# A spectral layer and a bilinear GLU on one core: where the first stage's odd folds run, and when its remaining features are split

## The chip, the cores and the metric

The kernel runs on one core of a Trainium2 chip. Its engines are TensorE (PE; PEld is its weight load), VectorE (DVE), ScalarE (ACT), GpSimd (POOL) and SyncE (SP), which issues most transfers. Each engine works through its own queue in order and meets the others through semaphores. The metric is the device time of one launch in microseconds (us); before the change it is 720.43 us, the median of 3 runs (720.38 to 720.56).

## The reference

`x` is 2048 rows of 640 float32 values. With `ln` a layer norm over the 640 values of a row (no gain, no bias):

```python
h   = x + irfft2(rfft2(ln(x)) * (w_r + 1j * w_i))       # w_r, w_i: 2048 x 321
h2  = h + ((ln(h) @ w_gate) * (ln(h) @ w_up)) @ w_down   # 640 x 1728, 1728 x 640
```

The first line is a global filter: a two-dimensional Fourier transform over rows and columns, a product with a learned complex filter, and the way back. The second is a gated unit without a nonlinearity.

## The kernel before, in words

The 2048 rows are 128 times 16: row 16p + t stands on partition p of tile t, so a tile (`XP[t]`, 640 values and one of padding) holds 128 rows, and there are 16 of them (`NT`). The transform over rows is split in the same way, into a 128-point part inside a tile and a 16-point part across tiles; the transform over the 640 columns uses its symmetry, so that columns are first added to and subtracted from their mirror images ("folds"), twice.

**Stage 1** (the loop at L262 to L292) goes over the tiles t = 0 to 15. For each tile:

- `odd(t)`, L178 to L181: 320 differences of mirrored columns, by GpSimd, from the raw tile. They need no layer-norm statistics, because a difference loses the mean.
- `even(t)`, three VectorE operations: L190 (322 sums of mirrored columns less twice the mean), L194 (66 second folds) and L195 (320 second folds). The last two read what `odd` and L190 wrote. The results lie in one of four slots of `fold` (`NR` = 4), so the folds of tile t + 4 wait until tile t's are used.
- `scale_c(t)`, L214: the 128 x 128 transform table times the rows' inverse deviation, by VectorE (by ScalarE for tile 0, L212).
- `s1_mm(t)`, L200 to L207: TensorE multiplies the folds with that table. Four blocks of 128 features go to one PSUM bank (L206), of which there are two in turn; the fifth block, the remaining features, goes to another (L207).
- The next turn of the loop reads the banks out: `s1_main` (L225, ScalarE) copies the four blocks; `s1_hi` (L220, ScalarE) writes the fifth block rounded to float32r into `s1r[:, 0]`, and `s1_lo` (L229, VectorE) the difference from the unrounded value into `s1r[:, 1]`.

The layer-norm statistics of tiles 0, 2, 3 and 6 to 9 are VectorE's (`bn_stats` at L131 and L132, `bn_aggr` at L133, two small operations at L137 and L138 for a group), those of tiles 1, 4, 5 and 10 to 15 ScalarE's (L146 and L147, then L149 on VectorE). After each group come a root on ScalarE (L156) and four small VectorE operations (L157 to L160) that give the inverse deviation. Lists say at which tile each operation is issued: `dve[t]` is zipped between the operations of `even(t)`, `acts[t]` follows `s1_hi` in ScalarE's queue, and `post[t]` holds the root. The order within every queue is the order of these calls; no planner changes it.

GpSimd's `odd(t + 1)` is issued in the turn of tile t, behind a one-element copy `hold` (L287) in the first two turns. `hold` reads the last element that L195 writes, so that the fold behind it starts when L195 of that turn is over.

**Stage 2** (from L315) takes 16 groups g (eight of the 128 outputs, from every tile): `d_mm(g)` multiplies the four main blocks (`s1`) and then the split fifth block (`s1r[:, 0]` twice, then `s1r[:, 1]`) with the column tables, `d_out(g)` (ScalarE, L328 to L331) copies the result, `s2_mm(g)` (L340) does the 16-point part, and VectorE's `filt(g)` multiplies with the filter. The filter and table loads on SP's queue follow these steps. The inverse transform, the second layer norm and the gated unit come after, with TensorE nearly always at work.

Of the kernel before, what the change touches and what calls it, by code (L numbers as in the profile page):

```python
# [11 lines left out]
F32 = mybir.dt.float32  # L12
F32R = mybir.dt.float32r
AF = mybir.ActivationFunctionType
OP = mybir.AluOpType

P = 128
S, D, NF, FF = 2048, 640, 321, 1728
NT = S // P
NG = 16  # L20
# [2 lines left out]
FW = (160, 193, 161, 161)  # L23
FOFF = (0, 160, 353, 514)
NR = 4
ON_ACT = (1, 4, 10, 14)
EPS = 1e-5


def view(t, offset, dims):  # L30
    return bass.AP(tensor=t.tensor, offset=t.offset + offset, ap=[list(t.ap[0])] + [list(d) for d in dims])


def f32(ap):
    return ap.bitcast(F32)


def zipped(main, side):
    n = len(main)
    for i, f in enumerate(main):  # L40
        f()
        for h in side[i * len(side) // n:(i + 1) * len(side) // n]:
            h()
# [3 lines left out]
def tile_spectral_glu(ctx: ExitStack, tc: tile.TileContext, x, wf, wgu, wlast, wdown, wdlast,  # L47
                      cc, ci, fmain, frem, imain, irem, mm, out):
    nc = tc.nc
# [3 lines left out]
    small = ctx.enter_context(tc.tile_pool(name="small", bufs=4))  # L53
    ctx.enter_context(tc.manual_schedule())

    tt, act = nc.vector.tensor_tensor, nc.scalar.activation
# [3 lines left out]
    def banks(key, name):  # L60
        if key in pools:
            open_pools[key].close()
        open_pools[key] = ExitStack()
        pools[key] = open_pools[key].enter_context(tc.tile_pool(name=name, bufs=2, space=bass.MemoryType.PSUM))
# [26 lines left out]
    XP = [keep.tile([P, D + 1], F32, name=f"x{t}") for t in range(NT)]  # L91
# [4 lines left out]
    def home(tag, shape, name, dt=F32):  # L96
        return keep.tile(shape, dt, tag=tag, name=name)
# [8 lines left out]
    frt = home("dA", [P, 2, 2, NQ], "frt", F32R)  # L106
    s1 = home("big", [P, 4, NG, P], "s1")
    s1r = home("wA", [P, 2, NG, P], "s1r", F32R)
    fold = home("qm", [P, NR * 1026 + 2 * D], "fold")
    wts = home("wB", [P, 3, 2, 2, NQ], "wts")  # L110
    bits = home("dB", [P, 2560], "bits")
# [9 lines left out]
    def moments(ts, junk=None, total=None):  # L121
        n = len(ts)
        m2 = small.tile([P, n], F32, tag="m2", name="m2")
        ve = small.tile([P, n], F32, tag="ve", name="ve")
        if junk is None:
            mv = small.tile([P, n, 2], F32, tag="mv", name="mv")

            def one(t, i):
                st = small.tile([P, 2, 6], F32, tag="st", name="st")
                return [  # L130
                    lambda: nc.vector.bn_stats(st[:, 0], X[t][:, 0:320]),  # L131
                    lambda: nc.vector.bn_stats(st[:, 1], X[t][:, 320:640]),  # L132
                    lambda: nc.vector.bn_aggr(mv[:, i], st),  # L133
                ]

            fs = [f for i, t in enumerate(ts) for f in one(t, i)]
            fs.append(lambda: nc.vector.tensor_scalar(m2, mv[:, :, 0], 2.0, None, op0=OP.mult))  # L137
            fs.append(lambda: nc.vector.tensor_scalar(ve, mv[:, :, 1], EPS, None, op0=OP.add))  # L138
            return m2, ve, fs
        sq = small.tile([P, n], F32, tag="sq", name="sq")  # L140
        fs = []
        if total is not None:
            fs.append(lambda: nc.vector.tensor_scalar(m2, total, 2.0 / D, None, op0=OP.mult))
        for i, t in enumerate(ts):
            if total is None:
                fs.append(lambda t=t, i=i: act(junk[i], X[t], AF.Identity, scale=2.0 / D, accum_out=m2[:, i:i + 1]))  # L146
            fs.append(lambda t=t, i=i: act(junk[i], X[t], AF.Square, bias=m2[:, i:i + 1], scale=-2.0,  # L147
                                           accum_out=sq[:, i:i + 1]))
        fs.append(lambda: nc.vector.tensor_scalar(ve, sq, 0.25 / D, EPS, op0=OP.mult, op1=OP.add))  # L149
        return m2, ve, fs  # L150
# [14 lines left out]
    def front(ts):  # L165
        n = len(ts)
        r = small.tile([P, n], F32, tag="r", name="r")
        junk = [fold[:, o:o + D] for o in (NR * 1026, NR * 1026 + D)]
        m2, ve, fs = moments(ts, junk * 2 if ts[0] in ON_ACT else None)
        for i, t in enumerate(ts):  # L170
            SC[t] = r[:, i:i + 1], m2[:, i:i + 1]
        return fs, inverse_root(ve, r, n)

    def folded(t):
        o = t % NR * 1026
        return fold[:, o:o + 642], fold[:, o + 642:o + 1026]

    def odd(t):  # L178
        f = folded(t)[0]
        nc.gpsimd.tensor_tensor(view(f, 0, [[160, 2], [1, 160]]), view(XP[t], 1, [[320, 2], [1, 160]]),  # L180
                                view(XP[t], 639, [[-320, 2], [-1, 160]]), op=OP.subtract)  # L181

    def even(t):
        f, j = folded(t)

        def both(n):
            return view(f, 0, [[320, 2], [1, n]]), view(f, 160, [[321, 2], [1, n]])

        return [
            lambda: nc.vector.scalar_tensor_tensor(view(f, 320, [[161, 2], [1, 161]]),  # L190
                                                   view(XP[t], 0, [[320, 2], [1, 161]]), SC[t][1],
                                                   view(XP[t], 640, [[-320, 2], [-1, 161]]),
                                                   op0=OP.subtract, op1=OP.add),
            lambda: tt(view(j, 33, [[-33, 2], [1, 33]]), *both(33), op=OP.add),  # L194
            lambda: tt(view(j, 64, [[1, 2], [2, 160]]), *both(160), op=OP.subtract),  # L195
        ]

    PS1, CR = {}, {}
# [10 lines left out]
    def scale_c(t):  # L209
        CR[t] = crs[t % 4]  # L210
        if t == 0:
            act(CR[t], cct, AF.Copy, scale=SC[t][0])  # L212
        else:
            nc.vector.tensor_scalar(CR[t], cct, SC[t][0], None, op0=OP.mult)  # L214

    def at(base, t):
        return view(base, 4 * t, [[64, 32], [1, 4]])

    def s1_hi(t):
        act(at(s1r[:, 0], t), PS1[t][1][:, 0:P].rearrange("p (g m) -> p g m", g=32), AF.Copy)  # L220

    def s1_main(t):
        n = 4 if t < NT - 1 else 2
        for c in range(0, 4, n):
            act(view(s1, 4 * t + 2048 * c, [[2048, n], [64, 32], [1, 4]]),  # L225
                PS1[t][0][:, c * P:(c + n) * P].rearrange("p (c g m) -> p c g m", c=n, g=32), AF.Copy)

    def s1_lo(t):
        tt(at(s1r[:, 1], t), PS1[t][1][:, 0:P].rearrange("p (g m) -> p g m", g=32), f32(at(s1r[:, 0], t)),  # L229
           op=OP.subtract)  # L230

    banks("a", "pone")
    dve = [[] for _ in range(NT)]
    acts = [[] for _ in range(NT)]
    post = {}

    def spread(fs, where, a, b):
        n = b - a + 1
        for k, f in enumerate(fs):
            t = a + k * n // len(fs)  # L240
            where[max(0, t)].append(f)

    warm = wk([P, P], "warm")
    nc.vector.memset(warm, 0.0)
# [4 lines left out]
    f1, c1 = front((1,))  # L249
    for f in f0:  # L250
        f()
    for first, n, a, b in ((2, 2, 0, 0), (4, 2, 0, 1), (6, 4, 1, 4), (10, 4, 4, 7), (14, 2, 8, 11)):
        fs, cs = front(range(first, first + n))
        if first in ON_ACT:
            spread(fs[:-1], acts, a, b)
            dve[b + 1].append(fs[-1])
        else:
            spread(fs, dve, a, b)
        post[first - 2] = cs[0]
        dve[first - 1] += cs[1:]  # L260
    odd(0)
    for t in range(NT):  # L262
        if t == 1:
            nc.gpsimd.dma_start(frt, frem)
        if t >= 1:
            s1_hi(t - 1)
            for f in acts[t]:
                f()
        if t:
            zipped(even(t), dve[t])  # L270
        else:
            e0 = even(0)
            for f in e0[:1] + c0 + e0[1:] + f1:
                f()
        if t >= 1:
            if t in post:
                post[t]()
            s1_main(t - 1)
            s1_lo(t - 1)
        else:  # L280
            scale_c(0)
            for f in c1[:1] + acts[0]:
                f()
            zipped(dve[0], c1[1:])
        if t + 1 < NT:
            if t < 2:
                nc.gpsimd.tensor_copy(small.tile([P, 1], F32, tag="hold", name="hold"), folded(t)[1][:, 383:384])  # L287
            odd(t + 1)
            scale_c(t + 1)
        if t == 0:  # L290
            post[t]()
        s1_mm(t)  # L292
    s1_main(NT - 1)
    s1_hi(NT - 1)
    s1_lo(NT - 1)

    WM, WI = {}, {}

# [11 lines left out]
    qr = home("qr", [P, 2, NT, P], "qr", F32R)  # L310
# [313 lines left out]
    for p in range(4):  # L624
        ts, t0 = (2 * p, 2 * p + 1), 2 * p + 2
        fs, cs = scale_shift(ts, [scrap] * 2, total[:, ts[0]:ts[0] + 2])
# [218 lines left out]
    for n, (blk, p) in enumerate(steps):  # L845
        if p == 6:
# [73 lines left out]
            if blk == 0:  # L920
                fs, cs = scale_shift(range(8, 16), None)
# [162 lines left out]
```

## Time and profile before

| what | before |
|---|---|
| median of 3 runs | 720.43 us |
| the profiled execution's own time | 720.28 us |
| its span (first to last instruction) | 718.5 us |
| TensorE busy in the span | 700.9 us |
| VectorE busy in the span | 466.9 us |
| VectorE busy between 7.94 and 47.78 us (stage 1) | 38.31 of 39.84 us |
| granted TensorE clock | 1.00 throughout |

The profiled execution took 1.78 us more than its span. In the timeline, a row gives the start from the beginning of the span, the duration, the engine, the line of the kernel, the operation, and the tiles written and read. Neighbouring rows of one engine can overlap by some hundredths of a microsecond, because an instruction is fetched and started while the one ahead is still writing; what an instruction costs its queue is therefore read from start to start, and not from its duration.

### The profile page before, as it was taken

What the parts mean: (1) busy time and instruction counts of PE and PEld (TensorE: products, weight loads), DVE (VectorE), ACT (ScalarE), POOL (GpSimd) and SP (SyncE); (2) the same over time, 40 slices, a digit from 0 to 9 for tenths busy, and PEclk for the clock granted to TensorE, in tenths of its full rate; (3) what the DMA queues carried; (4) which work ended last, traced back from release to release, by engine and by line L of the source; (5) the groups of instructions that cost most, each with busy time, mean ns of one, the idle gap of its engine ahead of it and who ended that gap; (6) DMA issues with size and microseconds to landing.
All of it is one profiled execution on the core that took longest, in us unless ns stands there. A gap on an engine that the chain in (4) does not pass through costs nothing.

```text
span 718.5 us, 10137 instructions
## 1 busy us (share of the span) xinstructions
PE 700.9 (98%) x3898; PEld 620.9 (86%) x3898; DVE 466.9 (65%) x810; ACT 252.8 (35%) x481; POOL 290.8 (40%) x269
## 2 busy tenths in 40 slices
PE   7899998999999999999999999999999999999998
PEld 7788997977888888989898989888898989898987
DVE  7967887798885656656555458565555555555454
ACT  4756666356541312222222255241222221222200
POOL 3310114332065445455464624055545455464600
PEclk9999999999999999999999999999999999999999
DMA  9405765000221212121110212311212121110203
GB/s 337 171 1 160 230 208 198 1 1 1 61 86 37 73 37 74 37 74 37 72 39 19 78 70 93 127 37 37 74 36 74 38 74 36 49 57 8 71 1 147
DMA packets 20928, 55.06 MB, mean 77 GB/s; under 512 B 2320, under 2 KB 6928, under 8 KB 20880
## 3 DMA queue, kind: packets, MB, share of 16 engines
q1 hardware_dynamic: 20304, 52.70, 21.5%
q0 software_dynamic: 288, 1.48, 0.6%
q8 instruction: 31, 0.51, 0.3%
q10 hardware_dynamic: 288, 0.23, 0.1%
q14 instruction: 17, 0.14, 0.1%
HBM read 49.16 MB, written 5.24 MB: 76 GB/s over the span
## 4 chain that ended last, share of the span: by engine, by line
PE 81%; DVE 13%; ACT 2%; issue 2%; DMA 1%; DVEq 0%; ACTq 0%
PE e L82 43%; PE y L82 26%; PE re L82 2%; PE im L82 2%; PE u L340 2%; PE eo L82 2%; DVE fold L190 2%; PE im L382 1%; DVE x L511 1%; DVE fold L195 1%; PE ir L382 1%; DMA x<-in_x_dram 1%; ACT zt L528 1%; DVE bits L214 1%; DVE x L513 1%
## 5 line engine op out<-in xcount | busy, mean ns | idle before, releaser
L82 PE MATMUL e<-xt,wst 128*128 128x512 f32 x864 | 206.8, 390 | 0.0
L82 PE MATMUL y<-wd,ht 128*128 128x320 f32 x1312 | 201.4, 310 | 1.2 <-DVE x L511 1.1
L82 PEld LDWEIGHTS y<-wd,ht 128*128 128x128 f32 x1312 | 195.3, 188 | 5.7 <-DVE x L511 2.7
L82 PEld LDWEIGHTS e<-xt,wst 128*128 128x128 f32 x864 | 160.7, 188 | 31.7
L511 DVE TENSOR_TENSOR x<-y,x 128x640 f32<-128x640 f32 x119 | 97.6, 822 | 70.4 <-PE y L82 70.1
L708 POOL TENSOR_TENSOR wst<-raw,wst 128x1024 fp32r<-128x1024 f32 x23 | 55.6, 2416 | 155.0 <-ACT wst L707 155.0
L724 POOL TENSOR_TENSOR wst<-raw,wst 128x896 fp32r<-128x896 f32 (+1 forms) x46 | 64.9, 1432 | 22.4 <-ACT wst L719 22.4
L82 PE MATMUL e<-t,wst 128*128 128x512 f32 x288 | 73.2, 389 | 0.1
L467 POOL TENSOR_TENSOR wd<-draw,wd 128x640 fp32r<-128x640 f32 x28 | 44.9, 1623 | 70.2 <-ACT wd L466 70.2
L820 ACT ACTIVATE ht<-e 128x512 fp32r<-128x512 f32 x24 | 14.4, 598 | 152.3 <-DVE e L819 152.3
L82 PEld LDWEIGHTS e<-t,wst 128*128 128x128 f32 x288 | 54.0, 188 | 11.7 <-DVE ht L659 0.5
L834 ACT ACTIVATE ht<-e 128x512 fp32r<-128x512 f32 x24 | 14.3, 598 | 114.1 <-DVE e L833 114.1
L82 PE MATMUL e<-xt,wdir 128*128 128x512 f32 x180 | 42.1, 392 | 0.2 <-DVE ht L663 0.2
L82 PEld LDWEIGHTS e<-xt,wdir 128*128 128x128 f32 x180 | 33.5, 188 | 7.5 <-issue 0.6
L707 ACT ACTIVATE wst<-raw 128x1024 fp32r<-128x1024 f32 x24 | 25.5, 1061 | 32.9 <-DMA raw<-in_wgu_dram 32.9
L206 PE MATMUL im<-bits,fold 128*128 128x128 f32 x192 | 30.1, 292 | 7.0 <-DVE fold L195 2.7
L82 PE MATMUL e<-ht,wst 128*128 128x512 f32 x144 | 36.5, 389 | 0.0
L813 DVE TENSOR_TENSOR u<-e,u 128x512 f32<-128x512 f32 x24 | 16.6, 692 | 29.5 <-PE e L82 29.4
L206 PEld LDWEIGHTS im<-bits,fold 128*128 128x128 f32 x192 | 24.6, 193 | 11.9 <-DVE fold L195 6.0
L82 PEld LDWEIGHTS e<-ht,wst 128*128 128x128 f32 x144 | 27.0, 188 | 5.6
L807 DVE TENSOR_TENSOR u<-e,p 128x512 f32<-128x512 f32 x24 | 16.6, 691 | 23.5 <-PE e L82 23.0
L412 POOL CAST qr<-bits 1x128 fp32r<-1x128 f32 x16 | 4.5, 280 | 67.6 <-DVE qr L407 66.7
(182 smaller groups left out, 1034.0 us busy)
## 6 DMA issues: line engine op xcount, KB each, us to landing
raw<-in_wgu_dram SPq DMA_DIRECT2D x24, 640.0 KB, 3.9
wts<-in_wf_dram SPq DMA_DIRECT2D x16, 644.0 KB, 4.0
draw<-in_wdown_dram SPq DMA_DIRECT2D x24, 320.0 KB, 4.6
x<-in_x_dram SPq DMA_DIRECT2D x16, 320.5 KB, 6.0
out_dram<-x SPq DMA_DIRECT2D x15, 320.0 KB, 2.2
bits<-in_mm_dram SPq DMA_DIRECT2D x32, 128.0 KB, 3.9
raw<-in_wgu_dram SPq DMA_DIRECT2D x4, 320.0 KB, 4.0
draw<-in_wdlast_dram SPq DMA_DIRECT2D x4, 320.0 KB, 2.9
```

Of the source, the lines that this page charges most:

```text
L82: nc.tensor.matmul(o, l, r, start=start, stop=stop, skip_group_check=True)
L190: lambda: nc.vector.scalar_tensor_tensor(view(f, 320, [[161, 2], [1, 161]]), view(XP[t], 0, [[320, 2], [1, 161]]), SC[t][1], view(XP[t], 6 ...
L206: nc.tensor.matmul(pm[:, k * P:(k + 1) * P], l, c, start=n == 0, stop=n == len(ls) - 1)
L340: nc.tensor.matmul(ps[h][:, 0:NQ], WM[g][0][:, h], T[g][:, h], start=True, stop=True)
L467: los.append(lambda r=r, a=a, b=b: engine.tensor_tensor(w[:, 1, a:b], r, f32(w[:, 0, a:b]), op=OP.subtract))
L511: tt(xv, ps[:, :, 0:320], xv, op=OP.add)
L707: act(wa[:, 0], stage[:, 0:1024], AF.Copy)
L708: ptt(wa[:, 1], stage[:, 0:1024], f32(wa[:, 0]), op=OP.subtract)
L724: ptt(ws[:, 1, o:o + b - a], stage[:, a:b], f32(ws[:, 0, o:o + b - a]), op=OP.subtract)
L807: tt(u2, o6, p1, op=OP.add)
L813: tt(u2, o5, u2, op=OP.add)
L820: act(hh[1], o3, AF.Copy)
```

## The change

Three things are changed, all in stage 1.

1. `AHEAD` = 7. GpSimd makes the odd folds of tiles 0 to 6 only, two tiles ahead: tile 0's at the start, tiles 1 and 2 behind a `hold` in turn 0, and tile t + 2 behind a `hold` in turn t for t = 1 to 4. The odd folds of tiles 7 to 15 become VectorE operations, issued in their own turn just ahead of `even(t)`.
2. The `bn_stats` and `bn_aggr` operations go to a list of their own, `stats[t]`, issued behind `even(t)` and no longer between its operations: one tile's statistics (tiles 6, 7, 8, 9) in each of turns 1 to 4. ScalarE's statistics of tiles 10 to 13 are spread over turns 2 to 7 instead of 4 to 7.
3. `s1_hi` and `s1_lo` go. ScalarE copies the fifth block unrounded into a new buffer `rest` (`s1_rest`, in the place of `s1_hi`). Behind the last tile, five pairs of a ScalarE copy and a VectorE subtraction (`rest_split`) split it, for groups 0 to 1, 2 to 3, 4 to 7, 8 to 11 and 12 to 15. `rest` lies where `qr` lies later.

```diff
+AHEAD = 7
+    rest = home("qr", [P, NG, P], "rest")
...
-    def odd(t):
+    def odd(t, engine):
         f = folded(t)[0]
-        nc.gpsimd.tensor_tensor(view(f, 0, [[160, 2], [1, 160]]), view(XP[t], 1, [[320, 2], [1, 160]]),
-                                view(XP[t], 639, [[-320, 2], [-1, 160]]), op=OP.subtract)
+        engine.tensor_tensor(view(f, 0, [[160, 2], [1, 160]]), view(XP[t], 1, [[320, 2], [1, 160]]),
+                             view(XP[t], 639, [[-320, 2], [-1, 160]]), op=OP.subtract)
...
-    def s1_hi(t):
-        act(at(s1r[:, 0], t), PS1[t][1][:, 0:P].rearrange("p (g m) -> p g m", g=32), AF.Copy)
+    def s1_rest(t):
+        act(at(rest, t), PS1[t][1][:, 0:P].rearrange("p (g m) -> p g m", g=32), AF.Copy)
...
-    def s1_lo(t):
-        tt(at(s1r[:, 1], t), PS1[t][1][:, 0:P].rearrange("p (g m) -> p g m", g=32), f32(at(s1r[:, 0], t)),
-           op=OP.subtract)
+    def rest_split(a, b):
+        act(s1r[:, 0, a:b], rest[:, a:b], AF.Copy)
+        tt(s1r[:, 1, a:b], rest[:, a:b], f32(s1r[:, 0, a:b]), op=OP.subtract)
...
-    for first, n, a, b in ((2, 2, 0, 0), (4, 2, 0, 1), (6, 4, 1, 4), (10, 4, 4, 7), (14, 2, 8, 11)):
+    for first, n, a, b in ((2, 2, 0, 0), (4, 2, 0, 1), (6, 4, 1, 4), (10, 4, 2, 7), (14, 2, 8, 11)):
         fs, cs = front(range(first, first + n))
         if first in ON_ACT:
-            spread(fs[:-1], acts, a, b)
+            for k, f in enumerate(fs[:-1]):
+                acts[a + k * (b - a + 1) // (2 * n)].append(f)
             dve[b + 1].append(fs[-1])
         else:
-            spread(fs, dve, a, b)
+            for k, f in enumerate(fs):
+                stats[min(b, a + k // 3 * (b - a + 1) // n)].append(f)
         post[first - 2] = cs[0]
         dve[first - 1] += cs[1:]
-    odd(0)
+    odd(0, nc.gpsimd)
     for t in range(NT):
         if t == 1:
             nc.gpsimd.dma_start(frt, frem)
         if t >= 1:
-            s1_hi(t - 1)
+            s1_rest(t - 1)
             for f in acts[t]:
                 f()
-        if t:
+            if t >= AHEAD:
+                odd(t, nc.vector)
             zipped(even(t), dve[t])
...
+        if t + 2 < AHEAD:
+            nc.gpsimd.tensor_copy(small.tile([P, 1], F32, tag="hold", name="hold"), folded(t)[1][:, 383:384])
+            for k in (1, 2) if t == 0 else (t + 2,):
+                odd(k, nc.gpsimd)
         if t >= 1:
+            for f in stats[t]:
+                f()
             if t in post:
                 post[t]()
             s1_main(t - 1)
-            s1_lo(t - 1)
...
-            zipped(dve[0], c1[1:])
+            zipped(stats[0], c1[1:])
         if t + 1 < NT:
-            if t < 2:
-                nc.gpsimd.tensor_copy(small.tile([P, 1], F32, tag="hold", name="hold"), folded(t)[1][:, 383:384])
-            odd(t + 1)
             scale_c(t + 1)
...
     s1_main(NT - 1)
-    s1_hi(NT - 1)
-    s1_lo(NT - 1)
+    s1_rest(NT - 1)
+    for a, b in ((0, 2), (2, 4), (4, 8), (8, 12), (12, 16)):
+        rest_split(a, b)
```

More of the change, by code (lines that the diff above doesn't have):

```diff
@@ L226, in s1_main @@
                 PS1[t][0][:, c * P:(c + n) * P].rearrange("p (c g m) -> p c g m", c=n, g=32), AF.Copy)
-    def s1_lo(t):
-        tt(at(s1r[:, 1], t), PS1[t][1][:, 0:P].rearrange("p (g m) -> p g m", g=32), f32(at(s1r[:, 0], t)),
-           op=OP.subtract)
+    def rest_split(a, b):
+        act(s1r[:, 0, a:b], rest[:, a:b], AF.Copy)
+        tt(s1r[:, 1, a:b], rest[:, a:b], f32(s1r[:, 0, a:b]), op=OP.subtract)
     banks("a", "pone")
-    dve = [[] for _ in range(NT)]
-    acts = [[] for _ in range(NT)]
+    dve, acts, stats = ([[] for _ in range(NT)] for _ in range(3))
     post = {}
[L237 to L241, printed above, removed]
     warm = wk([P, P], "warm")
```

## The prediction

> **What bounds the kernel now.** I read the engines' busy times first, then the chain of work that ended last, then busy time by stretch, and last the timeline of the first 50 us.
>
> ```profile
> PE 700.9 (98%) x3898; PEld 620.9 (86%) x3898; DVE 466.9 (65%) x810; ACT 252.8 (35%) x481; POOL 290.8 (40%) x269
> ```
>
> ```profile
> 7.94:47.78 39.84, 32.79 (x229) 28.02 (x227) 38.31 (x125) 25.35 (x69) 14.21 (x18) 1.00 0.47 179
> 49.05:718.50 669.45, 660.24 (x3626) 585.25 (x3626) 425.19 (x672) 223.74 (x405) 275.49 (x246) 1.00 0.21 69
> ```
>
> The rows of the second view are stretches; their busy columns are PE, PEld, DVE, ACT, POOL. Over the whole span TensorE is the bound, and from 49.05 us on it is busy 660.24 of 669.45 us. From 7.94 to 47.78 us it is VectorE, busy 38.31 of 39.84. The change lies between 7.94 and 47.78, so VectorE's order there is what has to be costed. How the stretch ends, by the chain:
>
> ```profile
> 45.57 0.51 DVE fold L195
> ...
> 47.09 1.51 PE im L206 x12
> ...
> 49.05 0.54 PE im L82 x2
> ```
>
> VectorE's folds (L195) release TensorE's last tiles, and stage 2 starts at 49.05. What follows is released by TensorE's own progress, so I take an earlier start of stage 2 one for one.
>
> A turn of VectorE's loop without GpSimd beside it, then one with it (GpSimd's row below belongs to it):
>
> ```profile
> 44.65 0.55 DVE L190 SCALAR_TENSOR_TENSOR fold<-x,m 128x322 f32<-128x322 f32 x1
> 45.31 0.23 DVE L194 TENSOR_TENSOR fold<-fold 128x66 f32<-128x66 f32 x1
> 45.57 0.49 DVE L195 TENSOR_TENSOR fold<-fold 128x320 f32<-128x320 f32 x1
> 45.98 0.28 DVE L229 TENSOR_TENSOR s1r<-ir,s1r 128x128 fp32r<-128x128 f32 x1
> 46.18 0.28 DVE L214 TENSOR_SCALAR bits<-cct,r 128x128 f32<-128x128 f32 x1
> 46.37 0.55 DVE L190 SCALAR_TENSOR_TENSOR fold<-x,m 128x322 f32<-128x322 f32 x1
> 47.29 0.49 DVE L195 TENSOR_TENSOR fold<-fold 128x320 f32<-128x320 f32 x1
> ```
>
> ```profile
> 10.77 0.55 DVE L190 SCALAR_TENSOR_TENSOR fold<-x,m 128x322 f32<-128x322 f32 x1
> ...
> 15.77 0.82 DVE L149 TENSOR_SCALAR ve<-sq 128x2 f32<-128x2 f32 x1
> ...
> 28.41 1.15 DVE L190 SCALAR_TENSOR_TENSOR fold<-x,m 128x322 f32<-128x322 f32 x1
> ...
> 29.93 0.49 DVE L195 TENSOR_TENSOR fold<-fold 128x320 f32<-128x320 f32 x1
> ...
> 30.73 1.15 DVE L190 SCALAR_TENSOR_TENSOR fold<-x,m 128x322 f32<-128x322 f32 x1
> ```
>
> ```profile
> 8.05 0.86 POOL L180 TENSOR_TENSOR fold<-x 128x320 f32<-128x320 f32 x1
> ...
> 13.00 3.56 POOL L180 TENSOR_TENSOR fold<-x 128x320 f32<-128x320 f32 x4
> ...
> 30.65 0.88 POOL L180 TENSOR_TENSOR fold<-x 128x320 f32<-128x320 f32 x1 [1.45 <-DVE fold L195]
> ```
>
> Alone, a turn takes 46.37 - 44.65 = 1.72 us. Beside a fold of GpSimd's, L190 takes 1.15 instead of 0.55 and the turn 30.73 - 28.41 = 2.32. Even L149, of two elements, takes 0.82 under the four folds from 13.00. VectorE waits for GpSimd's fold, about 0.6 us a time. `bn_stats` does not: here under GpSimd's fold at 8.05 it has its usual start-to-start times.
>
> ```profile
> 8.01 0.48 DVE L131 BATCH_NORM_STATS2 st<-x 128x6 f32<-128x320 f32 x1
> 8.41 0.48 DVE L132 BATCH_NORM_STATS2 st<-x 128x6 f32<-128x320 f32 x1
> ...
> 8.92 0.21 DVE L133 BATCH_NORM_AGGREGATE mv<-st 128x2 f32<-128x12 f32 x1
> 9.05 0.44 DVE L131 BATCH_NORM_STATS2 st<-x 128x6 f32<-128x320 f32 x1
> 9.41 0.14 DVE L158 SCALAR_TENSOR_TENSOR w<-r 128x1 f32<-128x1 f32 x1
> 9.46 0.49 DVE L132 BATCH_NORM_STATS2 st<-x 128x6 f32<-128x320 f32 x1
> ```
>
> **The change part by part.** I lay VectorE's new queue by start-to-start times: L190 to L194 0.66, L194 to L195 0.26, L195 to the next 0.41, L229 0.20, L214 0.19 (all from the free turn); L131 to L132 0.40, L132 to L133 0.51, L133 to the next 0.13, a small operation that nothing waits for 0.05 (9.41 to 9.46). Of the inverse deviation's chain, L157 and L158 fall into the waits ahead of L194 and L195, and the rest is read here:
>
> ```profile
> 34.65 0.49 DVE L195 TENSOR_TENSOR fold<-fold 128x320 f32<-128x320 f32 x1
> 35.06 0.15 DVE L159 TENSOR_TENSOR w<-w,ve 128x4 f32<-128x4 f32 x1
> 35.25 0.16 DVE L160 SCALAR_TENSOR_TENSOR r<-w,r 128x4 f32<-128x4 f32 x1
> ```
>
> L159 to L160, which needs it, is 0.19; I take 0.19 for whatever needs L160, and for L137 behind L133, too.
>
> *Turn 0.* GpSimd now makes folds 1 and 2 in one go from 8.05, so the second runs from 8.9 to about 9.8 (3.56/4 = 0.89 each). L158, queued for 9.41, reads two SBUF tensors as L190 does; no row shows it beside GpSimd. Bounds 0 and 0.4; I take that it waits until 9.8, since a two-element L149 waited. **+0.34**: L190 of tile 1 starts at 11.11 instead of 10.77.
>
> The Trainium skill (SBUF — State Buffer, "Who interferes with whom") says that a VectorE operation with two SBUF inputs and a GpSimd operation that reads SBUF shut each other out, and that whichever was issued first holds the port to its end. The trace agrees for L190 (1.15 against 0.55). It is the rule that speaks against making folds 1 and 2 in one go; without it the turn would cost 0 and the sum below be -4.44.
>
> *Turns 1 to 6* (before: 28.41 - 10.77 = 17.64). GpSimd's fold t + 2 starts some 0.2 after L195 ends (30.65 against 29.93 + 0.49; `hold` does the same) and ends 0.2 + 0.9 after it, so 1.6 after L195's start. `scale_c` is due behind the statistics, at 0.41 + 0.05 + 0.40 + 0.51 + 0.13 = 1.5 in turn 2 and 0.2 later in the others. I put 0.1 on turn 2. So turns 1 and 3, with chain and statistics, take 0.66 + 0.26 + 0.41 + 0.19 + 0.05 + 0.40 + 0.51 + 0.13 + 0.19 = 2.80; turn 2, with L149, 0.66 + 0.26 + 1.5 + 0.19 + 0.1 = 2.71; turn 4, with L137 and L138, 0.66 + 0.26 + 0.41 + 0.40 + 0.51 + 0.19 + 0.05 + 0.05 + 0.19 = 2.72; turn 5, chain without statistics, 0.66 + 0.26 + 0.41 + 0.19 + 0.19 + 0.19 = 1.90; turn 6, 0.66 + 0.26 + 0.41 + 0.19 = 1.52. Sum 14.45: **-3.19**. The stalls and the six L229 are worth more than that; some comes back, since statistics no longer fill the waits inside `even`.
>
> *Turns 7 to 15* (before: from 28.41 to L195's end at 47.29 + 0.49 = 47.78, so 19.37). No row shows the odd fold on VectorE. The nearest is L195, 320 elements of the same operation from SBUF to SBUF: 0.41. Lower bound L194's 0.26 (66 elements), upper bound L190's 0.66 (322 elements, mirrored columns too, with the wait of what needs it). I take 0.41, since L190 does not need the odd fold. A turn is 0.41 + 0.66 + 0.26 + 0.41 + 0.19 = 1.93; with L149 (turns 8, 12) 1.98; with the chain (9, 13) 1.93 + 0.19 + 0.19 = 2.31; turn 15, until L195 ends, 0.41 + 0.66 + 0.26 + 0.49 = 1.82. Four at 1.93, two at 1.98, two at 2.31 and 1.82 are 18.12: **-1.25**. Stalled turns get shorter (2.32 to 1.93), free ones longer (1.72 to 1.93).
>
> *ScalarE and TensorE* have to keep up.
>
> ```profile
> 29.16 0.28 ACT L220 ACTIVATE s1r<-im 128x128 fp32r<-128x128 f32 x1
> 29.33 0.73 ACT L146 ACTIVATE fold<-x 128x640 f32<-128x640 f32 x1
> ...
> 31.01 0.57 ACT L225 ACTIVATE s<-im 128x512 f32<-128x512 f32 x1
> ...
> 43.19 1.68 PE L206 MATMUL im<-bits,fold 128*128 128x128 f32 x12
> 44.93 1.93 PE L206 MATMUL im<-bits,fold 128*128 128x128 f32 x12
> ```
>
> A tile takes TensorE at most 44.93 - 43.19 = 1.74. The worst place is turn 5, which starts at 10.77 + 0.34 + 2.80 + 2.71 + 2.80 + 2.72 = 22.1. The root for tiles 6 to 9 needs L138 at the end of turn 4 and holds `s1_main(3)` until about 22.8; then come `s1_rest` (0.17), two statistics operations (31.01 - 29.33 = 1.68) and `s1_main(4)` (0.57), and only then, at 25.2, is there a bank for tile 6, over a microsecond later than VectorE has it ready. VectorE may run four slots ahead and does not stop. TensorE needs 10 x 1.74 = 17.4 from there, until 42.6. VectorE's last fold ends at 47.78 - 4.1 = 43.7, and TensorE's last tile ends a microsecond after it, as before. Cost 0, with 2 us to spare.
>
> *The split behind the last tile*, in the old timeline's times:
>
> ```profile
> 48.62 0.66 ACT L225 ACTIVATE s<-im 128x256 f32<-128x256 f32 x2 [0.73 <-PE im L206]
> 49.16 0.28 ACT L220 ACTIVATE s1r<-ir 128x128 fp32r<-128x128 f32 x1
> 51.25 0.43 ACT L328 ACTIVATE t<-re 64x322 f32<-64x322 f32 x1 [1.80 <-PE re L82]
> ```
>
> ```profile
> 50.17 0.19 PEld L82 LDWEIGHTS re<-frt,s1r 128*128 128x128 f32 x1
> ...
> 53.08 0.88 PEld L340 LDWEIGHTS u<-t,bits 128*128 128x128 f32 x4
> ```
>
> `s1_rest(15)` ends at 49.44 and the first copy of 256 columns at 49.8 (0.66/2 each), before TensorE first loads from `s1r` at 50.17; the lower part, which takes a subtraction of some 0.4 more, is read four matmuls later. The other copies (0.33 and three at 0.57) hold ScalarE until 51.8 at most, so `d_out(0)` is up to 0.55 late. Its four copies end at about 51.25 + 4 x 0.45 = 53.05, which becomes 53.6; TensorE reads the half they end in from 53.08 + 0.44 = 53.52. That is 0 to 0.1, and I take 0. Without this cover, if TensorE had to wait for all five pairs (51.8 and a subtraction of 512 columns, 0.49 x 512/320 = 0.8), it is 52.6 - 50.17 = 2.4.
>
> Sum: 0.34 - 3.19 - 1.25 + 0 = **-4.10**. 720.28 - 4.10 = 716.2 for the profiled execution, which lies 0.15 under the median of the runs, so **716.3 us**.
>
> **The rivals.**
>
> *B: the split gates stage 2.* `d_mm(0)` waits for all of `s1r`. For it: five writers of one tile, all behind the last tile. Against it: the slots of `fold` are pieces of one tile as well, and L190 at 44.65 wrote one while TensorE's matmuls from 43.19 read another. 716.3 + 2.4 = 718.7.
>
> *C: the early folds still stand in the way.* `hold` starts them too late, and each ends only after `scale_c` is due. In four turns at 0.6 at most 2.4, at half 1.2. For it: turn 2 has no slack. Against it: the others have 0.1 to 0.2. 716.3 + 1.2 = 717.5.
>
> *D: ScalarE or TensorE becomes the bound.* Were the 2 us to spare used up and as much again lost, 718.3. For it: the late bank for tile 6. Against it: that takes 0.4 us more in each of ten tiles.
>
> *E: slower.* One mechanism: the odd fold on VectorE, which reads the same tile forwards and backwards, runs far under L195's pace. Nine of them stand on the path; the gain is gone at 0.41 + 4.10/9 = 0.87 us each. At the stalled L190's 1.15 the time is 716.3 + 9 x 0.74 = 723.0. Against it: L190 reads forwards and backwards as well, in 0.55.
>
> *F: no change in the end.* The loop gets shorter, and something later that does not move with it (a transfer) takes the gain back: 720.4. Against it: TensorE's 660.24 busy of 669.45 us leave little room for such a wait.
>
> **How the numbers follow.** The forecast has 0.74 (its own range 715.0 to 717.4: L158 gives -0.34, an odd fold from 0.36 to 0.48 -0.45 to +0.6, the estimated waits 0.5 either way). B 0.09, C 0.07, D 0.04, F 0.04, E 0.02. The range is 715.0 to 718.7, which takes in B, C and D. The odd fold's outer bounds, 0.26 and 0.66, would give 715.0 and 718.6. A measurement of this kernel tells about 0.2% (1.4 us) from no change; faster by more than that are the forecast, B, C and D, 0.94; the same is F, 0.04; slower is E, 0.02.
>
> **What would show it.** Right: no L190 or L214 over 0.7 us; the odd folds on VectorE 0.4 us apart from L190; turns 7 to 14 of 1.9 to 2.3 us; stage 2's first matmul at about 44.9. L158 near 9.41 taking 0.5 shows turn 0. Wrong: TensorE idle at its first load from `s1r` (B), L214 of turns 1 to 4 long (C), VectorE waiting for TensorE's slots after turn 6 (D), an odd fold over 0.8 (E), or stage 2 four microseconds earlier and the end not (F).

## The result, and the profile after

The changed kernel takes 716.02 us (median of 6 runs, 715.52 to 716.83) against 720.44 for the kernel before (6 runs, 720.38 to 720.58); the ratio is 0.994, with a 95% interval of 0.9927 to 0.9952. The profiled execution has a span of 715.0 us and took 716.83. Line numbers have moved: L133 to L135 are the statistics (before L131 to L133), L182 the odd fold (L180), L192 the first even fold (L190), L196 and L197 the second folds (L194, L195), L216 the scaled table (L214), L222 the fifth block's copy (L220), L231 and L232 the split.

The page's busy times, and two stretches of the changed kernel that answer to those of before (columns PE, PEld, DVE, ACT, POOL):

```profile
PE 698.9 (98%) x3898; PEld 620.4 (87%) x3898; DVE 464.1 (65%) x808; ACT 254.6 (36%) x486; POOL 283.1 (40%) x263
```

```profile
7.94:43.24 35.30, 30.78 (x231) 27.56 (x230) 33.49 (x120) 25.15 (x71) 6.49 (x12) 1.00 0.53 202
44.51:715.00 670.49, 660.26 (x3626) 585.23 (x3626) 427.45 (x676) 225.99 (x410) 275.54 (x246) 1.00 0.20 68
```

VectorE's last even fold ends at 43.24 instead of 47.78, and stage 2 starts at 44.51 instead of 49.05. But the rest, which took 669.45 us before, takes 670.49 in this execution, with the same TensorE work (660.26 against 660.24). So 4.54 us were won in stage 1 and about 1.0 was lost later. The chain at the end of stage 1:

```profile
39.74 0.41 DVE fold L182
...
42.41 1.64 PE im L208 x12
...
44.08 0.39 ACT s L227
...
44.51 0.54 PE im L83 x2
```

It still goes from VectorE's folds to TensorE's last two tiles. From the end of VectorE's last fold (L197) to stage 2 it is 1.27 us, as before.

**Turn 0.** VectorE, and GpSimd's two folds:

```profile
9.22 0.44 DVE L133 BATCH_NORM_STATS2 st<-x 128x6 f32<-128x320 f32 x1
9.58 0.34 DVE L160 SCALAR_TENSOR_TENSOR w<-r 128x1 f32<-128x1 f32 x1
9.85 0.48 DVE L134 BATCH_NORM_STATS2 st<-x 128x6 f32<-128x320 f32 x1
...
11.14 0.55 DVE L192 SCALAR_TENSOR_TENSOR fold<-x,m 128x322 f32<-128x322 f32 x1
```

```profile
8.23 1.68 POOL L182 TENSOR_TENSOR fold<-x 128x320 f32<-128x320 f32 x2
```

L160, of one element, takes 0.34 instead of 0.14 and ends when GpSimd's second fold ends (9.91). The first tiles landed later in this execution: the first statistics started at 4.79 instead of 4.62, so 0.17 later. Less that, L192 at 11.14 is 0.20 later than before (10.77).

**Turns 1 to 4.** Turn 2, the tightest, with GpSimd's fold beside it:

```profile
15.31 0.49 DVE L133 BATCH_NORM_STATS2 st<-x 128x6 f32<-128x320 f32 x1
15.72 0.48 DVE L134 BATCH_NORM_STATS2 st<-x 128x6 f32<-128x320 f32 x1
16.23 0.21 DVE L135 BATCH_NORM_AGGREGATE mv<-st 128x2 f32<-128x12 f32 x1
16.35 0.23 DVE L216 TENSOR_SCALAR bits<-cct,r 128x128 f32<-128x128 f32 x1
16.50 0.55 DVE L192 SCALAR_TENSOR_TENSOR fold<-x,m 128x322 f32<-128x322 f32 x1
```

```profile
15.53 0.86 POOL L182 TENSOR_TENSOR fold<-x 128x320 f32<-128x320 f32 x1
```

The fold lies under the statistics from 15.53 to 16.39, and the scaled table, due at 16.35, is not held up. Before, beside a fold of GpSimd's, L190 took 1.15 (at 28.41) and the scaled table, L214, 0.87 (at 13.89).

**Turns 7 to 15**: the start of turn 7, then turn 10 for all, and the end of turn 15:

```profile
25.61 0.49 DVE L182 TENSOR_TENSOR fold<-x 128x320 f32<-128x320 f32 x1
...
31.70 0.48 DVE L182 TENSOR_TENSOR fold<-x 128x320 f32<-128x320 f32 x1
32.11 0.55 DVE L192 SCALAR_TENSOR_TENSOR fold<-x,m 128x322 f32<-128x322 f32 x1
32.69 0.23 DVE L196 TENSOR_TENSOR fold<-fold 128x66 f32<-128x66 f32 x1
32.95 0.49 DVE L197 TENSOR_TENSOR fold<-fold 128x320 f32<-128x320 f32 x1
33.36 0.28 DVE L216 TENSOR_SCALAR bits<-cct,r 128x128 f32<-128x128 f32 x1
33.56 0.49 DVE L182 TENSOR_TENSOR fold<-x 128x320 f32<-128x320 f32 x1
...
42.75 0.49 DVE L197 TENSOR_TENSOR fold<-fold 128x320 f32<-128x320 f32 x1
```

A turn takes 33.56 - 31.70 = 1.86 us, and the odd fold 0.41 of it.

**Where a microsecond went.** Both kernels load the first gate and up weights into a tile over the tables of the transform, as soon as the transform has read them. Before (the transfer's issue, its size and time to landing, and ScalarE's first use):

```profile
180.62 0.33 SPq L696 DMA_DIRECT2D raw<-in_wgu_dram  x1
```

```profile
raw<-in_wgu_dram SPq DMA_DIRECT2D x1, 640.0 KB, 3.9
```

```profile
185.16 1.05 ACT L707 ACTIVATE wst<-raw 128x1024 fp32r<-128x1024 f32 x1
```

After, where the second view, of 175.5 to 182 us, also shows the queue of instruction fetches:

```profile
176.09 0.33 SPq L697 DMA_DIRECT2D raw<-in_wgu_dram  x1
```

```profile
q8 instruction: 1, 0.02, 1.9%
...
raw<-in_wgu_dram SPq DMA_DIRECT2D x1, 640.0 KB, 5.5
```

```profile
181.68 1.06 ACT L708 ACTIVATE wst<-raw 128x1024 fp32r<-128x1024 f32 x1 [0.96 <-DMA raw<-in_wgu_dram]
```

The issue moved with stage 1, by 4.53 us. Before, the load landed 0.6 us ahead of its use (180.62 + 3.9 = 184.5 against 185.16). After, it took 5.5 instead of 3.9, and ScalarE waited 0.96 for it. VectorE's split of these weights and TensorE's next products are behind that: TensorE waited 1.23 us there (at 185.44) instead of 0.17 (at 188.91 before). Four of the kernel's six timed runs have spans of 713.7 to 714.0 us, which is 44.5 and the 669.45 of before, so they lost nothing behind stage 2; 714.8 and the profiled 715.0 are the other two.

### The profile page after: what moved, and what is told of

Read it like the earlier page. It is cut to its first block, busy times and chain, and to the rows that moved or that the text cites. A ratio compares the mean times of both kernels' runs of the same rounds, so it can differ in the third digit from the quotient of the medians.

```text
span 715.0 us, 10103 instructions
## 1 busy us (share of the span) xinstructions
PE 698.9 (98%) x3898; PEld 620.4 (87%) x3898; DVE 464.1 (65%) x808; ACT 254.6 (36%) x486; POOL 283.1 (40%) x263
## 4 chain that ended last, share of the span: by engine, by line
PE 84%; DVE 11%; ACT 2%; issue 1%; DMA 1%; DVEq 0%; ACTq 0%
PE e L83 45%; PE y L83 27%; PE re L83 2%; PE im L83 2%; PE u L341 2%; PE eo L83 2%; PE im L383 1%; DVE x L512 1%; DVE fold L197 1%; DVE fold L192 1%; PE ir L383 1%; DMA raw<-in_wgu_dram 1%; ACT zt L529 1%; DVE x L514 1%; DMA x<-in_x_dram 1%
## 5 line engine op out<-in xcount | busy, mean ns | idle before, releaser
L208 PE MATMUL im<-bits,fold 128*128 128x128 f32 x192 | 27.9, 287 | 4.5 <-DVE bits L216 1.6
L720 ACT ACTIVATE wst<-raw 128x896 fp32r<-128x896 f32 (+1 forms) x48 | 30.0, 674 | 2.7 <-POOL raw L714 1.9
```

Source lines behind the costliest of these rows:

```text
L208: nc.tensor.matmul(pm[:, k * P:(k + 1) * P], l, c, start=n == 0, stop=n == len(ls) - 1)
L720: act(ws[:, 0, o:o + b - a], stage[:, a:b], AF.Copy)
```

## The experiments

**early_undone.** The early part goes back to its old places; the late odd folds on VectorE and the split at the end stay, and so do ScalarE's earlier statistics of tiles 10 to 13.

```diff
-                stats[min(b, a + k // 3 * (b - a + 1) // n)].append(f)
+                dve[max(0, a + k * (b - a + 1) // len(fs))].append(f)
...
-        if t + 2 < AHEAD:
-            nc.gpsimd.tensor_copy(small.tile([P, 1], F32, tag="hold", name="hold"), folded(t)[1][:, 383:384])
-            for k in (1, 2) if t == 0 else (t + 2,):
-                odd(k, nc.gpsimd)
...
+            if t < 2:
+                nc.gpsimd.tensor_copy(small.tile([P, 1], F32, tag="hold", name="hold"), folded(t)[1][:, 383:384])
+            if t + 1 < AHEAD:
+                odd(t + 1, nc.gpsimd)
             scale_c(t + 1)
```

> The changed kernel with its early part undone: the odd folds of tiles 1 to 6 stay on GpSimd but are issued as before (fold t + 1 at the end of turn t), and the statistics go back between the operations of even(t). The folds of tiles 7 to 15 on VectorE and the split behind the last tile stay. Theory (VectorE's queue sets stage 1, and its start-to-start times add up): turns 1 to 6 took 17.64 us before; six L229 (1.2) and the two stalls by the folds of tiles 8 and 9 (1.1) are gone, so about 15.3 against 14.47 in the changed kernel, and turn 0 is 0.2 shorter without a second fold: stage 2 starts 0.6 later than in the changed kernel, at about 45.1. Rival (TensorE or ScalarE now sets the end, so that VectorE's early time is hidden): stage 2 starts within 0.2 of 44.5.

Stage 2 started at 45.21, 0.7 later than in the changed kernel; the median was 716.9 us (716.27 to 716.96; ratio to before 0.9949, 0.9937 to 0.9962). The theory's 0.6 nearly holds: turns 1 to 6 took 15.39 us (10.91 to 26.30) where it has 15.3. The stalls are back, on VectorE beside four folds of GpSimd's from 13.14 to 16.77:

```profile
14.04 1.15 DVE L192 SCALAR_TENSOR_TENSOR fold<-x,m 128x322 f32<-128x322 f32 x1
...
16.39 0.74 DVE L197 TENSOR_TENSOR fold<-fold 128x320 f32<-128x320 f32 x1
```

L197, a plain subtraction of two SBUF tensors, is stalled as well (0.74 against 0.49), which no row of before had shown. L151, which reads one tensor of two columns, waits too (0.82 at 15.11, instead of 0.16), as L149 did before.

**split_undone.** The fifth block is rounded and subtracted in every turn again.

```diff
     def s1_rest(t):
-        act(at(rest, t), PS1...
+        act(at(s1r[:, 0], t), PS1...
...
             s1_main(t - 1)
+            s1_lo(t - 1)
...
-    for a, b in ((0, 2), (2, 4), (4, 8), (8, 12), (12, 16)):
-        rest_split(a, b)
+    s1_lo(NT - 1)
```

> The changed kernel with the split behind the last tile undone: the fifth block is rounded and its lower part subtracted in every turn, as before. Theory (VectorE's queue): 15 subtractions at 0.20 us come back into VectorE's queue, 3.0 us, and stage 2 starts at about 47.5; the time rises by 3.0. Rival (TensorE at 1.74 to 1.97 us a tile already sets the second half): part of it is hidden, under 2 us.

Stage 2 started at 46.49 with the first statistics at 4.58, so 2.2 later than in the changed kernel (44.51 with 4.79); the median was 717.87 us (717.76 to 718.06; 0.9965, 0.9952 to 0.9977). Neither the theory's 3.0 nor the rival's less than 2 is what stage 2 shows. Eleven turns are 0.20 longer, as the theory has it, but three (5, 9 and 13) cost nothing, and the fifteenth subtraction lies behind the last fold. This is VectorE's own doing, not TensorE's. In turn 9 of this kernel the subtraction (L230) fills the wait of the scaled table (L215) for the inverse deviation (L161):

```profile
32.42 0.16 DVE L161 SCALAR_TENSOR_TENSOR r<-w,r 128x4 f32<-128x4 f32 x1
32.50 0.28 DVE L230 TENSOR_TENSOR s1r<-im,s1r 128x128 fp32r<-128x128 f32 x1
32.70 0.28 DVE L215 TENSOR_SCALAR bits<-cct,r 128x128 f32<-128x128 f32 x1
```

It is 0.28 from L161 to L215 with the subtraction between them, and in the changed kernel, where nothing lies between, it is 0.27 (31.23 to 31.50).

**all_gpsimd.** `AHEAD = 16`: every odd fold stays on GpSimd, two tiles ahead behind its hold.

```diff
-AHEAD = 7
+AHEAD = 16
```

> The changed kernel with AHEAD = 16: all odd folds on GpSimd, two tiles ahead, each behind its hold; from turn 5 on there are no statistics beside them. Theory (a VectorE operation with two SBUF inputs and a GpSimd fold shut each other out, whichever is first): the fold is asked for about 0.7 after the last even fold has started, when L192 of the next turn is already running; it starts when L192 ends and then holds L196 back for its 0.86 us. A turn is 1.52 + 0.75 = 2.3 instead of 1.86, over nine turns about 3.5 us, and stage 2 starts at 47.5 to 48.5. Rival (the folds are off the path, only the old place was wrong): turns of 1.5 to 1.75 us, set by TensorE, and stage 2 starts at 43.5 to 44.5.

Stage 2 started at 46.03, 1.5 later than in the changed kernel; the median was 717.5 us (717.38 to 717.57; 0.9959, 0.9946 to 0.9973). The sign and the mechanism are the theory's, the price is under half of it. VectorE at the end of turn 5 and in turn 7, and GpSimd's fold in turn 7:

```profile
23.81 0.84 DVE L216 TENSOR_SCALAR bits<-cct,r 128x128 f32<-128x128 f32 x1
...
26.09 0.55 DVE L192 SCALAR_TENSOR_TENSOR fold<-x,m 128x322 f32<-128x322 f32 x1
26.75 0.70 DVE L196 TENSOR_TENSOR fold<-fold 128x66 f32<-128x66 f32 x1
27.48 0.49 DVE L197 TENSOR_TENSOR fold<-fold 128x320 f32<-128x320 f32 x1
27.89 0.28 DVE L216 TENSOR_SCALAR bits<-cct,r 128x128 f32<-128x128 f32 x1
28.09 0.55 DVE L192 SCALAR_TENSOR_TENSOR fold<-x,m 128x322 f32<-128x322 f32 x1
```

```profile
26.25 1.11 POOL L182 TENSOR_TENSOR fold<-x 128x320 f32<-128x320 f32 x1
```

Here both wait: GpSimd's fold, asked for while L192 ran, takes 1.11 instead of 0.86, and L196, asked for while the fold ran, takes 0.70 instead of 0.23 and ends with it at about 27.4. The Trainium skill (SBUF — State Buffer, "Who interferes with whom") says that the order of issue decides who blocks; the trace shows both orders here, within 1.2 us (26.25 to 27.45).

This turn is 2.00 (26.09 to 28.09), not 2.3: the fold ends 0.72 after L192 (27.36 against 26.64) and not 0.86, and L196 is done 0.09 behind it. Nor does every turn pay. Behind the inverse deviation's chain (turns 5, 9 and 13) the fold meets the scaled table, which takes 0.84 instead of 0.28, and the next turn (6, 10 and 14) has no fold beside it and takes 1.51. That leaves 1.5 us in all.

**load_sooner.** The weights' tile is no longer a new tile in the tables' place, but the table tile itself, so that the load waits only for the reads of the part that it overwrites.

```diff
-    stage = home("stage", [P, 1448], "raw")
+    stage = tab
```

> The changed kernel with the first gate and up weights loaded over the table tile itself instead of a new tile at its place, so that the load waits only for the last read of the table under it and not for the transform that still reads the rest. Stage 1 is as in the changed kernel. Theory (the part of the gain that is missing in the profiled run, stage 2 4.54 earlier and the end 3.5 earlier, went to this load, which landed 5.5 us after its issue instead of 3.9): the load is issued some 10 us sooner, ScalarE does not wait for it, all timed runs lie close together at about 715.5, and span minus stage 2's start is about 669.4 as before the change. Rival (a spread between launches that has nothing to do with this load): the runs spread over 715.5 to 716.8 as those of the changed kernel do.

The median was 715.93 us (715.68 to 716.42; 0.9938, 0.9926 to 0.9951). The load went out at 165.57, and ScalarE did not wait for it:

```profile
165.57 0.33 SPq L697 DMA_DIRECT2D tab<-in_wgu_dram  x1
```

```profile
180.55 1.04 ACT L708 ACTIVATE wst<-tab 128x1024 fp32r<-128x1024 f32 x1
```

Span less stage 2's start is 713.9 - 44.42 = 669.5, as before the change. The spans of its five runs lie between 713.9 and 714.1; those of the changed kernel's six were 713.7 to 714.0 four times, and 714.8 and 715.0. The ten runs of four_scales and eight_scales, which load as early, have spans within 0.3 us too. So the theory holds for the span. The tight spans alone would not prove it, since the fifteen runs of early_undone, split_undone and all_gpsimd, with the load in its old place, also lie within 0.4 us of each other for each kernel; the 0.96 that ScalarE waits in one trace and not in the other is what shows it, for that execution. The theory does not hold for all of the spread: the time of a run less its span is 1.7 to 2.1 us in most runs of all kernels, but 2.3 to 2.4 in two of these five, 2.3 in one of the changed kernel's six, and 2.2 to 2.3 in four of early_undone's five. What lies outside the span is not in the trace, and this stays open. The median moved by 0.1 only, since most of the changed kernel's runs had not lost anything to the load (the median of the spans is 713.95 there and 713.9 here).

**four_scales** and **eight_scales.** On top of load_sooner, the scaled tables of tiles 10, 13, 14 and 15, or of all from 8 on, come from ScalarE. They ask which engine bounds the second half of stage 1 now. The edit of four_scales, whose condition is `t == 0 or t >= 8` in eight_scales:

```diff
-        if t == 0:
+        if t in (0, 10, 13, 14, 15):
             act(CR[t], cct, AF.Copy, scale=SC[t][0])
```

> The changed kernel with the first weight load issued sooner (as in load_sooner) and with the scaled tables of tiles 10, 13, 14 and 15 made by ScalarE instead of VectorE. Theory (VectorE's queue still sets the second half of stage 1): tables 13 and 15 give 0.20 us each, tables 10 and 14 also the 0.27 wait for the inverse deviation ahead of them, 1.3 us in all; TensorE, at 1.74 us a tile from tile 6's start at 25.1, can follow to about 42.8. Stage 2 starts at 43.1 to 43.4 instead of 44.42, and the time is about 714.7. Rival (TensorE or ScalarE sets the second half since the change): stage 2 starts at 44.2 to 44.5.

> As four_scales, but with the scaled tables of all tiles from 8 on made by ScalarE. Theory: VectorE's queue gets another 0.8 us shorter, to a stage 2 start of 42.3 to 42.6 if it alone counted; TensorE's own pace allows 42.8 at the earliest and ScalarE has statistics in turns 8 to 11, so the start moves by less than 0.4 against four_scales, and VectorE's queue has stopped being the bound. Rival (VectorE still alone): it moves by 0.8.

Stage 2 started at 43.48 and 43.49, with the first statistics at 4.64 and 4.86, so after them by 38.84 and 38.63, against 39.72 for load_sooner. The first step gave 0.9 of the expected 1.0 to 1.3, the second 0.2 of VectorE's 0.8. So VectorE's queue still was the bound in the changed kernel, by about a microsecond, and in eight_scales it is no longer. The chain of eight_scales runs over ScalarE and TensorE:

```profile
34.98 0.81 ACT fold L149 x2
35.78 0.49 ACT s L227
36.27 0.30 ACT bits L214
...
36.61 1.64 PE im L208 x12
```

The medians were 714.85 us (714.75 to 714.97; 0.9923, 0.991 to 0.9935) and 714.63 us (714.49 to 714.83; 0.992, 0.9906 to 0.9933). Both are about a microsecond faster than the changed kernel.

**one_pair.** The split behind the last tile in one piece.

```diff
-    for a, b in ((0, 2), (2, 4), (4, 8), (8, 12), (12, 16)):
-        rest_split(a, b)
+    rest_split(0, NG)
```

> The changed kernel with the split behind the last tile in one pair (one copy and one subtraction of all 2048 columns) instead of five. Theory (the split costs nothing because only the first 256 columns are needed at once): stage 2 starts at 44.5 as in the changed kernel, ScalarE's copy then takes about 2.2 us (0.55 for 512 columns) and VectorE's subtraction as long, so the lower part is there at about 49.3, where TensorE wants it at 46.2: some 3 us are lost, and the time is about 719. Rival (TensorE would have waited at this place anyway, for the copies of the first products): 1.5 us or less are lost, 717.5 at most.

Stage 2 started at 44.42, and TensorE then waited twice, 1.0 and 1.5 us:

```profile
46.81 0.42 PE L83 MATMUL re<-frt,s1r 128*128 128x322 f32 x1 [0.97 <-ACT s1r L231]
...
49.13 0.42 PE L83 MATMUL re<-frt,s1r 128*128 128x322 f32 x1 [1.46 <-DVE s1r L232]
...
51.57 1.25 PE L340 MATMUL u<-t,bits 128*128 128x322 f32 x4
```

The first 16-point products came at 51.57 instead of 48.69, 2.9 us later, which is the theory's 3. The median was 720.13 us (718.84 to 722.81; 0.9994, 0.9982 to 1.0006), a microsecond above the 719 that was expected. Its spans fall into groups: 716.9 to 717.0 five times, 718.1 to 718.4 four times, 720.5 and 720.9. The first group is near 713.9 + 2.9, with load_sooner's span for a load that lands in time. The profiled execution is of the second group: the weight load took 5.6 us there, ScalarE waited 1.05 for it, and again a fetch of instructions lies beside the load. In the profiles of before, early_undone, split_undone and all_gpsimd no such fetch lies beside it, and it took 3.9, 3.8, 4.0 and 3.8. The third group was not profiled.

## Why the prediction was right, and where it was not

- *The place and the sign.* VectorE's queue between 7.94 us and its last fold was the bound, and taking stalls and subtractions out of it moved stage 2 one for one: it starts 1.27 us after VectorE's last fold, before and after. Counted from the first statistics, stage 2 moved by 4.71 us (49.05 - 4.62 against 44.51 - 4.79); the sum had 4.10.
- *Turn 0.* Forecast +0.34, measured +0.20. The mechanism is the one that was costed, L160 waits for GpSimd's second fold, but it takes 0.34 and not 0.5: the two folds took 1.68 together and not 0.86 + 0.89, and the next statistics started a little before the fold's end (9.85 against 9.91).
- *Turns 1 to 6.* Forecast 14.45, measured 25.61 - 11.14 = 14.47. The sum is closer than its terms, by luck: turn 2 took 2.58 and not 2.71, as the 0.1 put on it was not needed, and turns 4 and 5 took 0.1 more each (2.82 and 1.99).
- *Turns 7 to 15.* Forecast 18.12, measured 43.24 - 25.61 = 17.63; this is the term that was mis-sized. The odd fold costs the 0.41 that was taken. What was wrong is L190 to L194, put at 0.66: behind an odd fold it is 0.58 (32.11 to 32.69), in all nine turns, so 0.7 us. Behind a scaled table it is 0.65 still (24.09 to 24.74). Why, the runs do not show. The wait of the scaled table for the inverse deviation is 0.27 and not 0.19, which gives 0.16 back.
- *ScalarE and TensorE.* Tile 6's matmuls started at 25.14; 25.2 was forecast for the bank. TensorE had caught up by tile 10, where it waited 0.20 for the odd fold. Rival D did not come. It may have been closer than the 2 us said: in eight_scales about one microsecond off VectorE's queue is all that the other engines allow, but there ScalarE makes eight more tables and stands on the chain with them, so what it would have allowed without them is not shown.
- *The split behind the last tile* costs nothing: ScalarE's five copies ran from 44.94 to 47.12 and put the first copies of `d_out` 0.4 late, and the 16-point products came at 48.69, 4.54 earlier, as all of stage 2. So rival B did not come. one_pair gives the price where the cover is gone: 2.9 us with one pair, where a wait for all five pairs had been put at 2.4.
- *Rival C* did not come either: no scaled table of turns 1 to 4 is stalled.
- *"One for one" behind stage 2* is the step that failed in part. In the profiled execution 1.0 of 4.54 us was lost to the weight load, and the mechanism is near rival F's: the load was issued 4.53 us earlier with the rest, but took 1.6 us longer to land, and so took back a fifth of the gain and not all. By the spans, one of the other five runs lost as much, and four lost nothing. Against F the prediction held TensorE's 660.24 busy of 669.45 us; that says how much waiting there is, not how close the next wait stands. The load's 0.6 us of cover could have been read in the trace of before.
- *The time.* 716.3 forecast, 716.02 measured. The number is closer than its parts, by luck: 0.6 more was won in stage 1 than costed, and the late load and the time outside the span took some of it back in part of the runs. Without them, 44.51 + 669.45 and 1.8 around the span make 715.8.

What each part is worth, from the undone ones, by stage 2's start after the first statistics: the early folds under the statistics 0.7 (early_undone, 40.45 against 39.72), the split behind the last tile 2.2, the late odd folds on VectorE rather than on GpSimd two tiles ahead 1.6 (all_gpsimd, 41.32). That is 4.5 of the 4.71, so the parts nearly add up. They need not do so exactly: all_gpsimd does not put the late odd folds back in their old place, one tile ahead, and ScalarE's earlier statistics were in all of these runs and were not undone apart.

## What to carry to other kernels

Where two engines shut each other out, an operation is best put beside those of the other engine that do not care (here the statistics), and where there are none, it can be cheaper to give it to the engine that would have waited: 0.41 us of VectorE's time replaced a stall of 0.6. When a gain is taken one for one through the rest of a kernel, look at the cover of every transfer behind it, not only at how busy the bound is. And once the bound is shortened, measure how far the next engine is: here moving four scaled tables to ScalarE gave 0.9 us more.

## What the runs showed of the hardware that was not expected

- A plain subtraction or addition of two SBUF tensors on VectorE is held up by a fold on GpSimd, as the fused form is: L197 0.74 against 0.49 (early_undone), L196 0.70 against 0.23 (all_gpsimd); and GpSimd's fold waits for VectorE in its turn, 1.11 against 0.86.
- A second SBUF tensor is not needed for it. The scaled table, a `TENSOR_SCALAR` with one tensor and one value per partition, takes 0.84 against 0.28 beside a fold (all_gpsimd), and L151, one tensor of two columns, 0.82 against 0.16 (early_undone). The statistics, with one tensor as well, take 0.48 beside a fold and without.
- A 640 KB weight load took 5.5 and 5.6 us to land in the two profiles in which an instruction fetch lay beside it, and 3.8 to 4.0 in the four others with the load at this place and the three that load sooner. The two go together in all nine profiles; that the fetch is the cause, or why it falls there in some executions, no run here shows.
- The same pair of dependent folds, L192 and L196, is 0.58 us apart behind an odd fold on VectorE and 0.65 behind a scaled table (changed kernel).
